# Three edits to a planned attention and two-layer kernel: work that POOL may take, copies left out, and sums that start without their scale

## The chip, the cores and the metric

The kernel runs on one core of a Trainium2 chip. The core has five engines with a queue each: TensorE (PE, with its weight loads shown apart as PEld), VectorE (DVE), ScalarE (ACT), GpSimd (POOL) and SyncE (SP), which here only issues DMAs. Each queue is worked off in order; an instruction at its head that waits holds up all that is behind it. The metric is the device time of one execution in microseconds (us); less is better. Three runs of the kernel before gave 1190.7, 1194.28 and 1189.9 us, median 1190.7.

## The reference

Three stages follow one another. Attention on 4 batches, 8 heads, 768 positions of 64 values, in chunks of 32 queries: each chunk sees 8 memory keys and its own keys with 16 to the left and 8 to the right, and the softmax is normalised. Its output, seen as 3072 tokens of 512 values, goes through a layer with a leaky rectifier, and that through a layer with a product of two branches:

```
a = np.exp(scores);  a = a / (np.sum(a, axis=-1, keepdims=True) + 1e-09)
x = (a @ v_full), all heads side by side: 3072 x 512
h = x @ w_in                                  # 512 x 2048
g = np.maximum(h, 0.0) + alpha * np.minimum(h, 0.0)
y = g @ w_out                                 # 2048 x 512
out = ((y @ w_a) * (y @ w_b)) @ w_o2          # 512 x 1536, twice, and 1536 x 512
```

## The kernel before

**Products.** Every large product runs in 16 bits with both factors split into an upper and a lower half (hi and lo): three matmuls, hi by hi, hi by lo and lo by hi, add up in PSUM (`gemm3`, lines 910 to 912). A split is one ACT instruction (hi, line 347) and one DVE instruction (lo = value times scale minus hi, line 351). The scale of a split is a power of two found from the largest magnitude of the data (`scale`, lines 299 to 330: a transpose on PE, line 310, and short DVE instructions from line 315 on).

**First stage.** The attention works on 24 units of 128 tokens. Of one unit (`attention`): k and q are turned on PE (lines 716 and 705), scores (740), the largest of a row (DVE, 756), exponentials with their sums (ACT, 766), the reciprocal of the sums (DVE, 774 and 777), the normalisation `norm` in two halves, each by DVE (782) or by ACT (788, four instructions), the turn of the normalised weights (PE, 792), their copy (`p_evac`, 645 on DVE or 647 on ACT), and the product with v (806). Two or four units make a block of x; `gemm1` multiplies it with `w_in` in 16 pieces. Each piece leaves PSUM through ACT (lines 927 and 930) and DVE (933) and is split: hi on ACT (939), lo on DVE (942, in `lo_`). `gemm2` needs all pieces of the block. Beside this the weights are made from 64-bit words (`chunk`): c0 on ACT (531), c1, c4, c2 and c3 on DVE (537 or 541, 546, 553, 560), then the scale and the split. For the 18 pieces of `w_a`, `w_b` and `w_o2` (`pair` is true) POOL forms sums of four quarters (`sums`, line 367), since the last layer multiplies with 7 products in place of 8 (Winograd's form), and the split parts go to DRAM.

**Second stage.** Six blocks of 512 tokens (`second`). For each of six pieces j, `pair` multiplies y with `w_a` and `w_b` and forms the product of both (`both`, line 1298), whose largest magnitude ACT takes (1304). From the six maxima comes one scale `sp` for the block (1253 to 1258). `operands` then forms the sums of the quarters of each piece (four instructions of line 367, one after the other, on POOL, in the last block on POOL or DVE) and splits pieces and sums (line 347 on ACT, 351 on DVE, two each). `output` multiplies with `w_o2`; each of its 7 products runs over all six pieces. The sums go into one of two buffers `s32`, which comes free when the piece is split; the split parts go into `pu`.

**What sets the order.** Nothing is ordered by hand. `Schedule` takes all operations with a rank, the data that they read and write, and an assumed cost on each engine that may run them. `emit` then always issues the operation that can start first by these assumed times, with ties by rank and cost, and writes it into the queue of the engine that it chose. The order of every queue is therefore fixed when the program is built.

## Time and profile before

| what | value |
|---|---|
| median of three runs | 1190.7 us (1189.9 to 1194.28) |
| the profiled execution | 1191.92 us |
| its span, first to last instruction | 1190.2 us |
| PE busy | 1126.7 us, 95% |
| DVE busy | 868.6 us, 73% |
| ACT busy | 604.7 us, 51% |
| POOL busy | 226.5 us, 19% |

The profiled execution took 1.7 us more than its span, which lies around the program, and is 1.2 us above the median. Busy time is counted once where instructions overlap. An idle time is put down to what ended it. TensorE's clock has two levels, 2.4 and 1.2 GHz; the profile gives the granted clock as a share of the higher one.

### The profile page before, as it was taken

Reading aid. Unit: us, or ns where it says so; the run is one execution under the profiler, and the core shown is the slowest. Engines: PE = TensorE matmul, PEld = TensorE weight load, DVE = VectorE, ACT = ScalarE, POOL = GpSimd, SP = SyncE. Lnnn points to the kernel's source line nnn. Section 1 sums busy time; section 2 is a strip of 40 time slices with the busy share of each in tenths; the row PEclk is TensorE's granted clock in tenths of the full one; section 3 lists DMA queues with packets and bytes.
Section 4 is the critical chain, followed back from the end, with each engine's and each line's share of the span. In section 5 each row is a group of like instructions: output and inputs, shape, how many; then the busy total and the mean of one; then the engine's idle time right before and its main releaser. Section 6 shows DMA issues by size and latency. Waiting matters only on the chain.

```text
span 1190.2 us, 23137 instructions
## 1 busy us (share of the span) xinstructions
PE 1126.7 (95%) x9304; PEld 811.2 (68%) x9304; DVE 868.6 (73%) x1533; ACT 604.7 (51%) x1326; POOL 226.5 (19%) x293
## 2 busy tenths in 40 slices
PE   4399999999999999999999999999999999999988
PEld 3278886555445554444444588888888888888877
DVE  6989998987998799335243187886867958858881
ACT  4689778975886698246253032433424423324340
POOL 1000012111112212100300010242433414234130
PEclk9589999999999999899999999999999999999999
DMA  9935664647635633530103052512513514315101
GB/s 263 258 81 139 154 191 127 186 132 219 200 103 167 194 127 106 179 140 32 50 10 133 27 190 90 188 66 94 191 54 112 173 37 156 130 52 187 63 36 37
DMA packets 162523, 150.93 MB, mean 127 GB/s; under 512 B 104032, under 2 KB 139888, under 8 KB 162416
## 3 DMA queue, kind: packets, MB, share of 16 engines
q1 hardware_dynamic: 162416, 149.45, 41.5%
q8 instruction: 73, 1.20, 0.4%
q14 instruction: 34, 0.28, 0.1%
HBM read 120.33 MB, written 29.10 MB: 126 GB/s over the span
## 4 chain that ended last, share of the span: by engine, by line
PE 74%; DVE 13%; ACT 6%; DMA 3%; SPq 2%; issue 2%; ACTq 0%; DVEq 0%
PE mm L910 23%; PE mm L912 23%; PE mm L911 23%; ACT sm L766 2%; PE pair L792 2%; DVE ghl L942 1%; DVE g L933 1%; DVE w L553 1%; PE mm L806 1%; DMA qt<-in_q_dram 1%; SPq L688 1%; DVE nm L756 1%; DVE w L560 1%; ACT sp L347 1%; ACT t L930 1%
## 5 line engine op out<-in xcount | busy, mean ns | idle before, releaser
L912 PE MATMUL mm<-xhl,w 128*128 128x512 f16 (+1 forms) x448 | 157.3, 351 | 1.9 <-DVE w L553 1.9
L910 PE MATMUL mm<-xhl,w 128*128 128x512 f16 (+1 forms) x448 | 157.6, 352 | 0.3 <-ACT t L930 0.2
L912 PE MATMUL mm<-ghl,w 128*128 128x512 f16 (+1 forms) x448 | 156.9, 350 | 0.9 <-DVE w L351 0.9
L911 PE MATMUL mm<-xhl,w 128*128 128x512 f16 (+1 forms) x448 | 157.4, 351 | 0.3 <-DVE xhl L351 0.3
L910 PE MATMUL mm<-ghl,w 128*128 128x512 f16 (+1 forms) x448 | 157.2, 351 | 0.0
L911 PE MATMUL mm<-ghl,w 128*128 128x512 f16 (+1 forms) x448 | 156.9, 350 | 0.0
L910 PE MATMUL mm<-units,w1b 128*128 128x256 f16 x560 | 153.4, 274 | 0.0
L911 PE MATMUL mm<-units,w1b 128*128 128x256 f16 x560 | 153.4, 274 | 0.0
L912 PE MATMUL mm<-units,w1b 128*128 128x256 f16 x560 | 153.3, 274 | 0.0
L912 PEld LDWEIGHTS <-w 128*128 128x128 f16 x896 | 88.2, 98 | 83.5 <-DVE w L553 2.2
L910 PEld LDWEIGHTS <-w 128*128 128x128 f16 x896 | 88.5, 99 | 75.5 <-issue 0.8
L911 PEld LDWEIGHTS <-w 128*128 128x128 f16 x896 | 88.3, 99 | 73.5 <-issue 1.7
L910 PE MATMUL mm<-w2b,w1b 128*128 128x256 f16 x504 | 137.4, 273 | 0.1
L912 PE MATMUL mm<-w2b,w1b 128*128 128x256 f16 x504 | 137.4, 273 | 0.0
L911 PE MATMUL mm<-w2b,w1b 128*128 128x256 f16 x504 | 137.4, 273 | 0.0
L910 PEld LDWEIGHTS <-w1b 128*128 128x128 f16 x1064 | 104.4, 98 | 13.0 <-DMA w1b<-wb_d 0.5
L911 PEld LDWEIGHTS <-w1b 128*128 128x128 f16 x1064 | 104.4, 98 | 12.7
L912 PEld LDWEIGHTS <-w1b 128*128 128x128 f16 x1064 | 104.4, 98 | 12.2
L367 POOL TENSOR_TENSOR raw<-w 128x256 f32<-128x256 f32 x18 | 16.1, 893 | 409.7 <-ACT raw L568 248.8
L933 DVE SCALAR_TENSOR_TENSOR g<-t,columns,g 128x512 f32<-128x512 f32 (+1 forms) x112 | 75.8, 683 | 24.3 <-ACT t L930 24.2
L942 DVE TENSOR_TENSOR ghl<-g,ghl 128x512 f16<-128x512 f32 (+1 forms) x112 | 70.8, 638 | 23.8 <-ACT ghl L939 23.4
L927 ACT ACTIVATE g<-mm 128x512 f32<-128x512 f32 (+1 forms) x112 | 60.5, 547 | 50.5 <-PE mm L912 48.4
(293 smaller groups left out, 2403.5 us busy)
## 6 DMA issues: line engine op xcount, KB each, us to landing
w1b<-wa_d SPq DMA_DIRECT2D x26, 896.0 KB
w1b<-wb_d SPq DMA_DIRECT2D x26, 896.0 KB
raw<-in_moe_w_out_dram SPq DMA_DIRECT2D x8, 1024.0 KB
kw<-in_k_dram SPq DMA_DIRECT2D x40, 176.0 KB
vw<-in_v_dram SPq DMA_DIRECT2D x40, 176.0 KB
qt<-in_q_dram SPq DMA_DIRECT2D x24, 256.0 KB
raw<-in_moe_w_a_dram SPq DMA_DIRECT2D x12, 512.0 KB
raw<-in_moe_w_b_dram SPq DMA_DIRECT2D x12, 512.0 KB
```

Of the source, the lines that this page charges most:

```text
L347: nc.scalar.activation(out=hi, in_=src, func=ACTF.Copy, scale=s)
L367: (nc.vector if e == "DVE" else nc.gpsimd).tensor_tensor(out=out_()[:, i], in0=x()[:, a], in1=y()[:, b], op=op)
L553: nc.vector.scalar_tensor_tensor(out=f, in0=lo, scalar=29, in1=f, op0=ALU.logical_shift_right, op1=ALU.bitwise_or)
L560: nc.vector.scalar_tensor_tensor(out=lo if nm == "w1" else f, in0=hi, scalar=KEEP, in1=f, op0=ALU.bitwise_and, op1=ALU.bitwise_or)
L766: nc.scalar.activation(out=sm.tile[:, o, g], in_=scored()[:, o, g], func=ACTF.Exp, bias=stat["nm"][:, i : i + 1], scale=1.0, accum_out=sta ...
L792: nc.tensor.transpose(out=heads(pp, P)[:KW, o, g], in_=sm.tile[:, o, g], identity=ident)
L910: nc.tensor.matmul(out=ps, lhsT=lh, rhs=rh, start=first and i == 0, stop=False)
L911: nc.tensor.matmul(out=ps, lhsT=lh, rhs=rl, start=False, stop=False)
L912: nc.tensor.matmul(out=ps, lhsT=ll, rhs=rh, start=False, stop=last and i == n - 1)
L927: nc.scalar.activation(out=g.tile[:, :n], in_=ps.tile[:, :n], func=ACTF.Relu, scale=E1)
L933: nc.vector.scalar_tensor_tensor(out=g.tile[:, :n], in0=t2.tile[:, :n], scalar=nal[:, m : m + 1], in1=g.tile[:, :n], op0=ALU.mult, op1=ALU ...
L942: nc.vector.tensor_tensor(out=ghl.tile[:, 1, m, d], in0=g.tile[:, :n], in1=ghl.tile[:, 0, m, d], op=ALU.subtract,)
```

## The change

There are three edits. `norm` may run on POOL as well as on DVE or ACT, and `lo_` of `gemm1` on POOL as well as on DVE, each with the planner's cost `pool(n)`. The inverse scale of the 18 pieces of `w_a`, `w_b` and `w_o2` is written straight to its place in `inv_w`, and the DVE copy that put it there (line 575) goes. In the last block of the second stage the sums of a piece wait for the piece and its maximum and no longer for the scale; the first two pieces take their sums' buffer from the larger `p32` buffers and their `pu` from `yu_slots`, the other four from `ring_slots`.

```diff
--- before.py
+++ after.py
@@ -510,7 +510,7 @@
         rk = raw_key(c) if nm == "w1" else (raw, 0)
         w32 = "w32w1" if nm == "w1" else Buf(w32_slots)
         fk = ("w32w1", c) if nm == "w1" else (w32, 0)
-        am, s, inv = (s_w1, s_w1, inv_w1) if nm == "w1" else (col(), col(), col())
+        am, s, inv = (s_w1, s_w1, inv_w1) if nm == "w1" else (col(), col(), inv_w[nm][:, c : c + 1] if pair else col())
         key = f"{nm}{c}"
 
         def load():
@@ -568,11 +568,8 @@
             nc.scalar.activation(out=t[:, :n], in_=w32.tile[:, :n], func=ACTF.Abs, accum_out=am)
 
         def after():
-            if nm == "w2":
-                r = slice(c % 2 * CR, (c % 2 + 1) * CR)
-                nc.vector.tensor_copy(out=inv_w2[r, c // 2 : c // 2 + 1], in_=inv[r])
-            else:
-                nc.vector.tensor_copy(out=inv_w[nm][:, c : c + 1], in_=inv)
+            r = slice(c % 2 * CR, (c % 2 + 1) * CR)
+            nc.vector.tensor_copy(out=inv_w2[r, c // 2 : c // 2 + 1], in_=inv[r])
 
         sd.op("SP", dma(n * 8 * P), load_rank, load, (), [rk])
         sd.op("ACT", act(n), rank, c0, [rk], [fk])
@@ -591,7 +588,7 @@
             sd.op("ACT", act(n, 2), rank, sizes, [fk], [rk, (key + "am", 0)])
             scale(
                 lambda: am, s, inv, [(key + "am", 0)], [(key + "s", 0), (f"inv_{nm}{c}", 0)],
-                rank=rank - 0.3, after=[after],
+                rank=rank - 0.3, after=[after] if nm == "w2" else [],
             )
         def scaled():
             src = [rk, ("s_w1", 0)] if nm == "w1" else [(w32, 0), (key + "s", 0)]
@@ -778,8 +775,8 @@
 
         def norm(e, o):
             rs = stat["rs"][:, o * HP : (o + 1) * HP]
-            if e == "DVE":
-                nc.vector.tensor_tensor(
+            if e != "ACT":
+                (nc.vector if e == "DVE" else nc.gpsimd).tensor_tensor(
                     out=sm.tile[:, o], in0=sm.tile[:, o],
                     in1=rs[:, :, None].to_broadcast([P, HP, KW]), op=ALU.mult,
                 )
@@ -839,7 +836,7 @@
         sd.op("DVE", 0.09, rank, part_of, [], [(sm, 2)])
         for o in range(2):
             sd.op(
-                None, {"DVE": dve(n), "ACT": 4 * act(KW, 1) + 0.15}, rank, lambda e, o=o: norm(e, o),
+                None, {"DVE": dve(n), "ACT": 4 * act(KW, 1) + 0.15, "POOL": pool(n)}, rank, lambda e, o=o: norm(e, o),
                 [(sm, 2), (sm, 0)], [(sm, ("n", o))],
             )
             sd.op("PE", 4 * pe(P, 2), prank, lambda o=o: p_turn(o), [(sm, ("n", o))], [(pp, o)])
@@ -938,8 +935,8 @@
         def hi_():
             nc.scalar.copy(out=ghl.tile[:, 0, m, d], in_=g.tile[:, :n])
 
-        def lo_():
-            nc.vector.tensor_tensor(
+        def lo_(e):
+            (nc.vector if e == "DVE" else nc.gpsimd).tensor_tensor(
                 out=ghl.tile[:, 1, m, d], in0=g.tile[:, :n], in1=ghl.tile[:, 0, m, d],
                 op=ALU.subtract,
             )
@@ -955,7 +952,9 @@
         sd.op("ACT", act(n), er, below, [(ps, 0)], [(t2, 0)])
         sd.op("DVE", dve(n, pointers=1), er, both, [(t2, 0), ("alpha", 0)], [(g, 0)])
         sd.op("ACT", act(n), er, hi_, [(g, 0)], [(ghl, ("h", m, c0))])
-        sd.op("DVE", dve(n), er, lo_, [(g, 0), (ghl, ("h", m, c0))], [(ghl, (m, c0))])
+        sd.op(
+            None, {"DVE": dve(n), "POOL": pool(n)}, er, lo_, [(g, 0), (ghl, ("h", m, c0))], [(ghl, (m, c0))]
+        )
 
     def gemm2(jb, m, ghl, c0, n, iy, rank):
         ps, y32 = Buf(mm_slots), Buf(g_slots)
@@ -1172,13 +1171,14 @@
                 keys += [("yd", j, m) for m in range(KD)]
         return keys
 
-    def operands(r, b, h, s, reads, cost):
-
-        o = Buf(s32_slots)
+    def operands(r, b, h, s, reads, cost, ready=None, slots_=None):
+
+
+        o = Buf(slots_ or s32_slots)
         unit = lambda: b.tile
-        others = lambda: o.tile
-
-        sd.op("POOL", 0.0, r, lambda: None, reads, [(h, "held")], holds=[h])
+        others = lambda: o.tile[:, :3]
+
+        sd.op("POOL", 0.0, r, lambda: None, reads if ready is None else ready, [(h, "held")], holds=[h])
         sums(
             r, b, o, [(b, 0), (h, "held")], [],
             [
@@ -1261,10 +1261,14 @@
             lambda: am1, sp, io, [(f"amp1{jb}", 0), ("ratio", 0)], [(f"sp{jb}", 0)], after=after
         )
 
-        pu = {j: Buf((ring_slots if i < 4 else yu_slots) if last_ else pu_slots) for i, j in enumerate(js)}
+        pu = {j: Buf((yu_slots if i < 2 else ring_slots) if last_ else pu_slots) for i, j in enumerate(js)}
         cost = {"POOL": pool(HT), "DVE": dve(HT)} if last_ else {"POOL": pool(HT)}
         for j in js:
-            operands(r, ps[j], pu[j], lambda j=j: spj[:, j : j + 1], [(f"sp{jb}", 0), (ps[j], 0)], cost)
+            operands(
+                r, ps[j], pu[j], lambda j=j: spj[:, j : j + 1], [(f"sp{jb}", 0), (ps[j], 0)], cost,
+                [(ps[j], 0), ("amp", jb, j)] if last_ else None,
+                p32_slots if last_ and j in list(js)[:2] else None,
+            )
         for tt in range(HT // P):
             output(jb, tt, pu, io, r + 30)
 
```

Since the planner chooses anew at each step, the queues change everywhere in the first stage. Three places follow. The lines of `attention` and `gemm1` have numbers lower by 3 in the changed kernel.

PE, where the first stage's products begin, in the kernel before; `qt` is a unit's q, `xhl` the split x and `w_94` the split `w_in`:

```order
L740 MATMUL pair<-kT,qT 64x96 x16
L310 MATMUL mm<-ident,columns 128x128 x2
L705 MATMUL mm<-ident,qt 128x128 x4
L910 LDWEIGHTS w_94
L910 MATMUL mm<-xhl,w_94 128x256
L911 LDWEIGHTS w_94
L911 MATMUL mm<-xhl,w_94 128x256
L912 LDWEIGHTS w_94
L912 MATMUL mm<-xhl,w_94 128x256
```

The same place in the changed kernel:

```order
L737 MATMUL pair<-kT,qT 64x96 x16
L310 MATMUL mm<-ident,columns 128x128 x2
L907 LDWEIGHTS w_94
L907 MATMUL mm<-xhl,w_94 128x256
L908 LDWEIGHTS w_94
L908 MATMUL mm<-xhl,w_94 128x256
L909 LDWEIGHTS w_94
L909 MATMUL mm<-xhl,w_94 128x256
```

The turn of the third unit's q, which stood ahead of the first product, now stands behind its twelve matmuls (four groups of three).

POOL, behind the masks that it writes at the start, in the kernel before; `raw` and `w_2098` hold a piece of `w_a`:

```order
L294 MEMSET mask_88 32x32
L298 MEMSET mask_88 32x8
L367 TENSOR_TENSOR raw<-w_2098 128x256
L367 TENSOR_TENSOR raw<-w_2098,raw 128x256
L367 TENSOR_TENSOR w_2098<-w_2098 128x256
```

The same place in the changed kernel, up to the first sum:

```order
L294 MEMSET mask_88 32x32
L298 MEMSET mask_88 32x8
L779 TENSOR_TENSOR sm<-sm,rs 128x384 x3
L939 TENSOR_TENSOR ghl<-g,ghl 128x256 x3
L779 TENSOR_TENSOR sm<-sm,rs 128x384 x2
L939 TENSOR_TENSOR ghl<-g,ghl 128x256 x5
L779 TENSOR_TENSOR sm<-sm,rs 128x384
L939 TENSOR_TENSOR ghl<-g,ghl 128x256 x5
L779 TENSOR_TENSOR sm<-sm,rs 128x384
L939 TENSOR_TENSOR ghl<-g,ghl 128x256 x8
L779 TENSOR_TENSOR sm<-sm,rs 128x384 x3
L367 TENSOR_TENSOR raw<-w_2067 128x256
```

In the whole program POOL gets 23 halves of the normalisation (line 779, 384 elements to a partition) and 43 lower halves (line 939; 21 of 256 elements and 22 of 512). DVE loses 12 halves of the normalisation, the same 43 lower halves and the 18 copies; ACT loses 44 instructions of the normalisation (11 halves). Three copies of k move from ACT to DVE, and three copies of weights from DVE to ACT.

DVE behind the last block's scale (line 1258), in the kernel before; `x_6475`, `quarters`, `w1b` and `xhl` as inputs of line 367 are pieces, `s_...` the buffers of sums, `cb` an output of the block before:

```order
L1258 TENSOR_TENSOR columns<-columns 128x1
L421 SCALAR_TENSOR_TENSOR cb<-mm_12826,columns,g 128x512
L367 TENSOR_TENSOR s_12936<-quarters 128x256
L427 SCALAR_TENSOR_TENSOR cb<-mm_12826,columns,cb 128x256
L367 TENSOR_TENSOR x_6475<-x_6475 128x256
L367 TENSOR_TENSOR s_12916<-s_12916,x_6475 128x256
L367 TENSOR_TENSOR s_12936<-s_12936,quarters 128x256
L433 SCALAR_TENSOR_TENSOR cb<-mm_12891,columns,cb 128x512
L351 SCALAR_TENSOR_TENSOR w1b<-x_6475,columns,w1b 128x1024
L415 SCALAR_TENSOR_TENSOR cb<-mm,columns,cb 128x256
L351 SCALAR_TENSOR_TENSOR w1b<-s_12916,columns,w1b 128x768
L351 SCALAR_TENSOR_TENSOR w1b<-quarters,columns,w1b 128x1024
```

The same place in the changed kernel:

```order
L1258 TENSOR_TENSOR columns<-columns 128x1
L421 SCALAR_TENSOR_TENSOR cb<-mm_12784,columns,g 128x512
L427 SCALAR_TENSOR_TENSOR cb<-mm_12784,columns,cb 128x256
L351 SCALAR_TENSOR_TENSOR units<-x_6412,columns,units 128x1024
L433 SCALAR_TENSOR_TENSOR cb<-mm_12858,columns,cb 128x512
L351 SCALAR_TENSOR_TENSOR units<-w2b,columns,units 128x768
L351 SCALAR_TENSOR_TENSOR units<-quarters,columns,units 128x1024
L415 SCALAR_TENSOR_TENSOR cb<-mm,columns,cb 128x256
L351 SCALAR_TENSOR_TENSOR units<-ghl,columns,units 128x768
L351 SCALAR_TENSOR_TENSOR w1b<-x_6412,columns,w1b 128x1024
L409 SCALAR_TENSOR_TENSOR g<-mm,columns,cb 128x256
L351 SCALAR_TENSOR_TENSOR w1b<-s_12671,columns,w1b 128x768
```

Behind the scale DVE had twelve sums of line 367 among its twelve splits; now it has three, all further down, and four pieces have their sums ahead of the scale.

## Rows read from the trace of the kernel before

**Rows 1.** Windows: stretch, length, PE, PEld, DVE, ACT, POOL busy, PE clock, DMA

```profile
0.00:62.00 62.00, 25.77 (x231) 18.96 (x232) 48.94 (x86) 35.01 (x85) 4.97 (x41) 0.74 0.95 256
62.00:500.00 438.00, 420.44 (x3694) 264.93 (x3693) 377.80 (x722) 332.17 (x868) 64.68 (x73) 0.99 0.54 152
300.00:360.00 60.00, 55.43 (x399) 29.49 (x398) 56.16 (x97) 51.98 (x130) 7.40 (x8) 1.00 0.52 149
1152.00:1164.00 12.00, 7.45 (x43) 4.92 (x41) 7.80 (x11) 4.00 (x5) 1.55 (x2) 0.72 0.10 35
```

**Rows 2.** Waits of PE, 0 to 62 us: us in total, times, longest

```profile
PE pair L792 <- DVE sm L782: 11.9, 2, 7.0
PE mm L705 <- DMA qt<-in_q_dram: 10.3, 1, 10.3
```

**Rows 3.** Timeline, DVE and PE before the first product: start, duration, instruction

```profile
21.51 0.69 DVE L645 COPY pT<-pair 96x512 f32<-96x512 f32 x1 [1.11 <-PE pair L792]
...
34.42 1.03 DVE L782 TENSOR_TENSOR sm<-sm,rs 128x384 f32<-128x384 f32 x2
...
57.64 1.42 DVE L351 SCALAR_TENSOR_TENSOR xhl<-x,columns,xhl 128x512 f16<-128x512 f32 x2 [0.24 <-ACT xhl L347]
...
60.24 1.09 PE L705 MATMUL mm<-ident,qt 128*128 128x128 f32 x4 [10.33 <-DMA qt<-in_q_dram]
```

**Rows 4.** Groups by form, DVE and ACT, whole span: busy us, mean ns | idle

```profile
L942 DVE TENSOR_TENSOR ghl<-g,ghl 128x512 f16<-128x512 f32 x80 | 58.1, 728 | 23.0 <-ACT ghl L939 22.6
...
L782 DVE TENSOR_TENSOR sm<-sm,rs 128x384 f32<-128x384 f32 x32 | 17.5, 571 | 0.6
...
L942 DVE TENSOR_TENSOR ghl<-g,ghl 128x256 f16<-128x256 f32 x32 | 12.7, 415 | 0.8 <-ACT ghl L939 0.8
...
L575 DVE COPY columns<-columns 128x1 f32<-128x1 f32 x18 | 2.4, 134 | 0.0
```

**Rows 5.** Groups by form, ACT, whole span

```profile
L788 ACT ACTIVATE sm<-sm,rs 128x96 f32<-128x96 f32 x64 | 18.7, 377 | 5.4 <-DVE rs L777 5.4
```

**Rows 6.** Groups by form, POOL, whole span

```profile
L367 POOL TENSOR_TENSOR raw<-w,raw 128x256 f32<-128x256 f32 x36 | 33.1, 920 | 1.3
...
L367 POOL TENSOR_TENSOR s<-s,x 128x256 f32<-128x256 f32 x12 | 8.7, 725 | 0.0
```

**Rows 7.** Timeline, POOL, in the last block

```profile
1136.36 0.72 POOL L367 TENSOR_TENSOR s<-quarters,s 128x256 f32<-128x256 f32 x1
1139.57 1.70 POOL L367 TENSOR_TENSOR s<-x 128x256 f32<-128x256 f32 x1 [2.48 <-DVE w1b L351]
```

**Rows 8.** Timeline, DVE, behind the last block's scale

```profile
1132.91 0.15 DVE L1258 TENSOR_TENSOR columns<-columns 128x1 f32<-128x1 f32 x1
...
1133.64 0.41 DVE L367 TENSOR_TENSOR s<-quarters 128x256 f32<-128x256 f32 x1
...
1136.47 1.70 DVE L351 SCALAR_TENSOR_TENSOR w1b<-x,columns,w1b 128x1024 f16<-128x1024 f32 x1
...
1139.41 1.27 DVE L351 SCALAR_TENSOR_TENSOR w1b<-quarters,columns,w1b 128x1024 f16<-128x1024 f32 x1
1142.26 0.48 DVE L409 SCALAR_TENSOR_TENSOR g<-mm,columns,cb 128x256 f32<-128x256 f32 x1 [1.57 <-ACT cb L406]
...
1154.74 0.43 DVE L367 TENSOR_TENSOR s<-xhl,s 128x256 f32<-128x256 f32 x1
...
1157.21 1.28 DVE L351 SCALAR_TENSOR_TENSOR units<-xhl,columns,units 128x1024 f16<-128x1024 f32 x1
```

**Rows 9.** Timeline, PE, at the last block's first output product

```profile
1156.42 0.39 PE L912 MATMUL mm<-units 128*128 128x256 f16 x1 [3.25 <-DVE units L351]
...
1158.54 0.39 PE L912 MATMUL mm<-units 128*128 128x256 f16 x1 [1.30 <-DVE units L351]
...
1163.15 0.27 PE L910 MATMUL mm<-units,w1b 128*128 128x256 f16 x1
1163.26 0.27 PE L911 MATMUL mm<-units,w1b 128*128 128x256 f16 x1
```

## The prediction

> **What bounds the kernel.** I read the windows first, by stage, for where PE is not busy; then the waits of PE; then the timeline at the two largest; then the groups that the edits touch. PE works 1126.7 of 1190.2 us, so a change of its helpers can return no more than the 63.5 us in which it stands still, and what a low clock costs. Of the idle time 36.2 us lie before 62 us (62.0 less 25.8), 17.6 between 62 and 500 (438.0 less 420.4), and 4.6 between 1152 and 1164 [rows 1]. Before 62 us two waits stand out: 11.9 us for normalised weights and 10.3 us for the third unit's q [rows 2]. At the end it is two waits for the last piece's splits, 3.25 and 1.30 us [rows 9]. Of DVE the reader is to see that it is the nearest second: 377.8 of 438 us in the first stage, and 56.2 of 60 in the stretch from 300 us, where PE lost 4.6 us [rows 1]. POOL has room: 64.7 of 438.
>
> **The end: sums without the scale.** Before, nothing of the six pieces could start until the scale was there at 1133.06 (1132.91 and 0.15), and the first half of the last piece was ready at 1158.49 (1157.21 and 1.28) [rows 8]. In these 25.4 us DVE did twelve splits, eight instructions of the output of the block before, and twelve sums, of which the first and the last took 0.41 and 0.43 us [rows 8]. In the new order three of the twelve sums are left behind the scale. Nine sums at 0.42 are 3.8 us; some of them were held up beside POOL, so I take 4.2. The other way to the same place: DVE waited 1.57 us for a product of PE at 1142.26 [rows 8], and PE's place in that product does not change, so the new order reaches that point, does five splits ahead of it where it did three, and goes on at 1142.7. Behind it stand seven splits (three of 1.27 us as at 1139.41, four of three quarters of that size, 0.95: 7.6), four outputs (two as at 1142.26, 0.48, two twice as wide, counted at 0.7: 2.4) and the three sums (1.3): 11.3 us, which would end at 1154.0 were nothing waited for, the first half of the last piece 0.95 earlier. But the two last pieces take their sums' buffers from the third and the fourth, so five POOL instructions of 0.73 [rows 6] stand in between, in a chain with those three sums; I give this 1.2 us. So 1154.3, which is 4.2 earlier. PE comes to that operand at 1153.17 (1156.42 less 3.25), and its two waits of 4.55 us become one of about 1.1: 3.4 gained. From both sides: 0, if the POOL chain is late by 4 us more, and 4.55.
>
> Behind the wait PE ran at the lower clock level, until 1163: between 1152 and 1164 the granted clock is 0.72 and 43 matmuls took 7.45 us [rows 1]; at the step of 0.11 us between 1163.15 and 1163.26 [rows 9] they take 4.7. That is 2.7 us, which goes if the level holds through a wait of 1.1 us. No row shows that for certain; I take two thirds, 1.8. The end gives 5.2 us, with 0 and 7.2 as its bounds. The held buffers cost nothing that I can see: `yu_slots` has two units free in the last block, and the ring's units come free with the pieces whose product is done. What the earlier sums stand in front of on POOL is only other sums; on DVE one of 0.42 us comes ahead of the last `both`, and the transpose for the scale is tied to its place in PE's queue anyway.
>
> **The start: norm on POOL.** Before the first product DVE loses one copy of weights (0.69) and one of two normalisations (1.03 for both) [rows 3]: 1.2 us. The split x was ready at 59.06 (57.64 and 1.42), but PE stood at the turn of q until 60.24, for its DMA [rows 3]. In the new order twelve matmuls come first, and the q is there by the time that they end. So PE starts at 59.1 if DVE gains nothing and at 57.9 if it gains all: 1.1 to 2.3 us earlier. POOL's own halves are longer than those they replace (below), and one of them is in the chain of 11.9 us [rows 2], so the lower bound is 0; I take 1.6.
>
> **The middle: DVE and ACT against POOL.** Removed from DVE: 22 lower halves of 0.728, 21 of 0.415, 12 normalisations of 0.571 and 18 copies of 0.134 [rows 4]: 16.0, 8.7, 6.9 and 2.4, in all 34.0 us. From ACT: 44 of 0.377 [rows 5], 16.6 us. The copies that change sides are three each way, about nothing. Added to POOL: the trace has no such instruction of POOL. Its sums of 256 elements take 0.725 us undisturbed and 0.92 in the first stage [rows 6]. For 512 elements the bounds are 0.73 (no growth) and 1.84 (twice the slow one); I take 1.4, and for 384 by the same line 1.05. So 21 at 0.73, 22 at 1.4 and 23 at 1.05: 70.3 us, with which POOL is busy some 135 of 438 us, which it can be. No queue is held up for that but POOL's own: sums of the weight pieces stand behind it, and they have until the second stage.
>
> But the two engines get in each other's way. At 1136.36 POOL worked for 0.72 us, and DVE's split of 1136.47 took 1.70 in place of 1.27; at 1139.41 DVE's split began first, took its 1.27, and POOL's sum of 1139.57 took 1.70 in place of 0.72 [rows 7, 8]. Each time the later one ends as if it had begun when the other was done. On the average POOL pays 0.2 us an instruction (0.92 less 0.725) [rows 6]; for DVE I take as much, an estimate: 66 new instructions, 13 us. DVE keeps a relief of 21 us in 378, ACT 17 in 332.
>
> The Trainium skill says this harder (SBUF — State Buffer, section "Who interferes with whom"): DVE and GpSimd share a pair of ports that is an exclusive lock, a DVE instruction with two inputs in SBUF takes part in it when GpSimd reads SBUF, and the one that comes second blocks fully. The two collisions above agree. By that rule every microsecond moved to POOL could cost DVE as much, which is the second rival below.
>
> PE's 17.6 us of waits in the middle are many small ones. With less on DVE and ACT they shrink; with a slower engine inside the attention's chain and a wholly new order some come anew. Bounds: 10 us better (more than half gone) and 20 worse (below). I take 1.5 better, close to nothing, since the nearest row, the stretch with PE 55.4 and DVE 56.2 of 60 [rows 1], shows that both bind there.
>
> **The sum.** 5.2, 1.6 and 1.5 are 8.3 us. The profiled execution took 1191.9 (span 1190.2 and 1.7 around it): 1183.6. It lay 1.2 above the median of its runs, so the time to compare with that median is 1182.4. About 0.5%, 6 us, is what can be told from no change: below 1184.7 is faster, above 1196.7 slower.
>
> **Rivals.** *The order wins more.* The end returns all of 7.2, the start 2.3, the middle 5: 14.5 us, so 1176. For it: planner and chip agree on a DVE with 9% less to do. Against: PE's queue is as strict as before.
>
> *POOL shuts DVE out.* One mechanism, in the first stage: POOL's 66 instructions hold what DVE's two-input instructions need. If DVE pays the full 70.3 us, it goes from 377.8 to 414 of 438, 95%, about PE's own share. The stretch from 300 us shows the price of that: DVE at 94%, PE idle 4.6 of 60 [rows 1]; over 438 us that is 33.6 in place of 17.6, 16 worse, and if half of POOL's longer latencies come on top, 20. With the gains of 6.8 elsewhere it ends 9 to 13 above 1190.7, near 1201. It decides from the point where DVE pays more than 34.0 us, 0.5 an instruction. For it: the collisions are complete. Against: POOL's sums have paid only 0.2 each, and DVE's reductions and its readings of PSUM go on beside POOL.
>
> *The end does not come.* The chain of POOL sums for the last two pieces is so late that PE waits as long as before and the clock falls as before; start and middle give 3.1 or are lost to a new wait: 1188 to 1191, no change. For it: the two `s32` buffers tie the last pieces to the splits of the third and fourth. Against: nine sums fewer on the engine that was late.
>
> **From here to the chances.** The forecast 0.43, the larger gain 0.21, no gain at the end 0.26, POOL's lock 0.10. The forecast's own range, 1179 to 1187, lies for three quarters below 1184.7. Faster: 0.33 and 0.21, 0.54. Same: the rest of the forecast and the third rival, 0.36. Slower 0.10. The range for 8 in 10 leaves out most of the lock and the far end of the larger gain: 1174 to 1193.
>
> **What would show it.** Right at the end: PE's two waits by the last units' splits of 1.5 us or less in sum, and three sums on DVE behind the scale. Right at the start: the first product near 58.5 us. Right in the middle: DVE near 357 us of the same 438, its two-input instructions hardly longer on the average, PE idle near 16. Wrong: lower halves on DVE that last over 1 us beside POOL's, POOL's own at over 2 us, PE waiting for normalised weights from POOL, or the lower clock level still behind the last scale.

## The result, and the profile after

The changed kernel takes 1204.4 us in the median of four runs, against 1190.5; the ratio of the runs is 1.0101, with a 95% interval from 1.0086 to 1.0117. The forecast was 1182.4, with a range of 1174 to 1193. The kernel became slower where it was to become faster. The profiled execution has a span of 1202.3 us, 12.1 more than before.

The windows of the changed kernel, columns as in [rows 1]:

```profile
0.00:62.00 62.00, 29.19 (x243) 21.09 (x244) 49.31 (x84) 35.90 (x87) 8.86 (x44) 0.67 0.95 256
62.00:500.00 438.00, 406.10 (x3568) 255.25 (x3567) 377.47 (x638) 324.21 (x819) 141.95 (x134) 0.98 0.54 149
300.00:360.00 60.00, 55.82 (x399) 29.76 (x396) 54.78 (x89) 43.92 (x110) 28.35 (x25) 0.97 0.63 189
1152.00:1164.00 12.00, 12.00 (x113) 10.76 (x111) 10.62 (x13) 8.02 (x9) 1.30 (x1) 1.00 0.12 45
```

PE is busy through the whole of the last stretch, at the full clock; before it had 7.45 of 12 at 0.72. From 62 to 500 it stands still for 31.9 us (438.0 less 406.1) where it was 17.6. DVE is as busy as before, 377.5 and 377.8, with 84 instructions fewer. Two places of PE's timeline show both ends, the number in brackets being the idle time before:

```profile
57.08 0.37 PE L907 MATMUL mm<-xhl,w 128*128 128x256 f16 x1 [10.19 <-ACT xhl L347]
...
1172.88 0.28 PE L909 MATMUL mm<-units,w1b 128*128 128x256 f16 x1 [0.66 <-DVE w1b L351]
```

PE goes on at 57.08, 3.2 us earlier than at 60.24 [rows 3]; the two waits of 4.55 us by the last splits [rows 9] have become one of 0.66. So start and end gave more than forecast, the end some 6.6 (3.9 of waits and the 2.7 of the low clock), and about 22 us were lost between (12.1, 3.2 and 6.6). The waits of PE from 62 to 500 us (in total, times, longest) say where:

```profile
PE mm L310 <- ACT raw L568: 13.2, 13, 2.3
PE pair L789 <- DVE sm L779: 3.1, 3, 1.3
PE mm L310 <- DVE columns L874: 3.0, 3, 1.4
...
PE pair L789 <- POOL sm L779: 0.7, 1, 0.7
```

In the kernel before the first of these was:

```profile
PE mm L310 <- ACT raw L568: 2.0, 3, 0.8
```

It is the transpose of a weight piece's maximum (`scale`), which stands in PE's queue and waits for ACT's maximum, and this for DVE's four instructions that put the piece's words together. PE hardly waits for POOL. The groups of DVE by form answer to [rows 4] (busy us, mean ns | idle):

```profile
L939 DVE TENSOR_TENSOR ghl<-g,ghl 128x512 f16<-128x512 f32 x58 | 42.9, 739 | 36.4 <-ACT ghl L936 36.4
...
L779 DVE TENSOR_TENSOR sm<-sm,rs 128x384 f32<-128x384 f32 x20 | 13.6, 679 | 0.5
L939 DVE TENSOR_TENSOR ghl<-g,ghl 128x256 f16<-128x256 f32 x11 | 6.6, 605 | 0.0
```

The groups of POOL by form answer to [rows 6]:

```profile
L367 POOL TENSOR_TENSOR raw<-w,raw 128x256 f32<-128x256 f32 x36 | 35.0, 973 | 1.3
L939 POOL TENSOR_TENSOR ghl<-g,ghl 128x512 f16<-128x512 f32 x22 | 30.3, 1376 | 165.5 <-ACT ghl L936 165.3
L779 POOL TENSOR_TENSOR sm<-sm,rs 128x384 f32<-128x384 f32 x23 | 26.4, 1149 | 155.4 <-DVE rs L774 66.1 <-DMA vw<-in_mem_v_dram 25.2 <-ACT raw L568 17.1
L939 POOL TENSOR_TENSOR ghl<-g,ghl 128x256 f16<-128x256 f32 x21 | 20.7, 988 | 48.9 <-ACT ghl L936 48.8
```

POOL's 66 instructions took 77.4 us (estimated: 70.3). DVE's normalisation went from 571 to 679 ns and its lower halves of 256 from 415 to 605. One place shows how such a delay reaches PE, in the timeline of all engines:

```profile
377.01 0.74 DVE L930 SCALAR_TENSOR_TENSOR g<-t,columns,g 128x512 f32<-128x512 f32 x1
...
377.21 3.65 POOL L939 TENSOR_TENSOR ghl<-g,ghl 128x512 f16<-128x512 f32 x2 [1.28 <-ACT ghl L936]
...
379.77 1.64 DVE L930 SCALAR_TENSOR_TENSOR g<-t,columns,g 128x512 f32<-128x512 f32 x1
...
381.45 0.62 ACT L936 CAST ghl<-g 128x512 f16<-128x512 f32 x1 [0.56 <-DVE g L930]
...
384.03 1.04 ACT L568 ACTIVATE raw<-w 128x1024 bf16<-128x1024 f32 x1
...
385.22 0.32 PE L310 MATMUL mm<-ident,columns 128*128 128x128 f32 x1 [2.33 <-ACT raw L568]
```

The same DVE instruction takes 0.74 us and, next to POOL's pair, 1.64; ACT idles 0.56 us before its upper half, the maximum stands behind three more instructions on ACT, and PE waits 2.33 us. So of these 2.33 us, 0.56 come visibly from this one delay; for the rest the place shows no single cause. The first section of the profile's page counts it all up:

```profile
PE 1131.8 (94%) x9304; PEld 811.7 (68%) x9304; DVE 871.3 (72%) x1455; ACT 598.3 (50%) x1282; POOL 315.6 (26%) x364
```

### The profile page after: what moved, and what is told of

It is laid out like the page before. It is cut to its first block, busy times and chain, and to the rows that moved or that the text cites. A ratio compares the mean times of both kernels' runs of the same rounds, so it can differ in the third digit from the quotient of the medians.

```text
span 1202.3 us, 23165 instructions
## 1 busy us (share of the span) xinstructions
PE 1131.8 (94%) x9304; PEld 811.7 (68%) x9304; DVE 871.3 (72%) x1455; ACT 598.3 (50%) x1282; POOL 315.6 (26%) x364
## 4 chain that ended last, share of the span: by engine, by line
PE 68%; DVE 20%; ACT 6%; issue 4%; DMA 2%; SPq 1%; POOL 0%; ACTq 0%; DVEq 0%; POOLq 0%
PE mm L907 22%; PE mm L908 22%; PE mm L909 22%; DVE g L930 3%; DVE w L560 2%; DVE w L553 2%; ACT sm L763 2%; DVE w L541 1%; DVE sp L351 1%; DVE nm L753 1%; PE pair L789 1%; DVE w L546 1%; DVE ghl L939 1%; DVE columns L812 1%; DMA kw<-in_k_dram 1%
## 5 line engine op out<-in xcount | busy, mean ns | idle before, releaser
L907 PE MATMUL mm<-xhl,w 128*128 128x512 f16 (+1 forms) x448 | 158.9, 355 | 10.4 <-ACT xhl L347 10.2
L939 POOL TENSOR_TENSOR ghl<-g,ghl 128x512 f16<-128x512 f32 (+1 forms) x43 | 51.0, 1186 | 214.4 <-ACT ghl L936 214.2
L930 DVE SCALAR_TENSOR_TENSOR g<-t,columns,g 128x512 f32<-128x512 f32 (+1 forms) x112 | 83.7, 753 | 29.6 <-ACT t L927 29.4
L936 ACT CAST ghl<-g 128x512 f16<-128x512 f32 (+1 forms) x112 | 62.0, 561 | 52.0 <-DVE g L930 51.8
```

Source lines behind the costliest of these rows:

```text
L907: nc.tensor.matmul(out=ps, lhsT=lh, rhs=rh, start=first and i == 0, stop=False)
L930: nc.vector.scalar_tensor_tensor(out=g.tile[:, :n], in0=t2.tile[:, :n], scalar=nal[:, m : m + 1], in1=g.tile[:, :n], op0=ALU.mult, op1=ALU ...
L936: nc.scalar.copy(out=ghl.tile[:, 0, m, d], in_=g.tile[:, :n])
L939: (nc.vector if e == "DVE" else nc.gpsimd).tensor_tensor(out=ghl.tile[:, 1, m, d], in0=g.tile[:, :n], in1=ghl.tile[:, 0, m, d], op=ALU.sub ...
```

## The experiments

Three theories. A: POOL's instructions hold DVE up, and that is the loss. B: the loss is in the new order, whatever runs where. C: the results come later from POOL than from DVE. Times are medians; "before" was run on the same chip each time, with medians from 1192.1 to 1193.4, so ratios are what to compare. One per cent is 11.9 us.

**The edits one by one.** First the last block's edit alone in the kernel before (`operands` and `pu` as changed, all else old):

> The kernel before with the edit of the last block alone; the queues of the first stage are those of before, instruction for instruction. The changed kernel's trace had no wait and no low clock left at the end, 4.55 and 2.7 us less. So every theory expects 1183 to 1185, about 6.6 us below before. If it is 1187 or more, part of what vanished at the end of the changed kernel vanished because its last block came at another time, and the middle then cost less than 24 us.

1186.5 us, ratio 0.9952 (0.9937 to 0.9967): 5.7 us gained, on the end alone; the 6.6 of the trace lie within the interval. Next the changed kernel with fewer choices for POOL:

```diff
-None, {"DVE": dve(n), "ACT": 4 * act(KW, 1) + 0.15, "POOL": pool(n)}, rank, lambda e, o=o: norm(e, o),
+None, {"DVE": dve(n), "ACT": 4 * act(KW, 1) + 0.15}, rank, lambda e, o=o: norm(e, o),
-None, {"DVE": dve(n), "POOL": pool(n)}, er, lo_,
+"DVE", dve(n), er, lo_,
```

Both lines changed:

> The changed kernel without POOL as a choice for the normalisation and the lower halves; the copies stay out and the sums of the last block begin early. The planner orders the first stage anew, as it does for any change. Theory A (POOL's instructions hold DVE up) expects 1182 to 1186. Theory B (a new order is itself worse, whatever runs where) expects a loss of some size here too, 1190 or more.

The first alone:

> The changed kernel with POOL as a choice for the lower halves alone: 57 of them (25 of 256, 32 of 512 elements), at the changed kernel's durations 25 x 0.99 and 32 x 1.38, 69 us of POOL. The changed kernel lost about 24 us in the middle with 77 us on POOL. Theory A (the loss goes with POOL's time, since DVE is held up) expects 21 us of loss, 1200 to 1205. Theory C (POOL's long instruction lies in the chain of the attention, from the sums to the turn of the weights) expects most of the loss gone: 1183 to 1190.

The second alone:

> The changed kernel with POOL as a choice for the normalisation alone: 22 halves of 1.15 us, 25 us of POOL. Theory A expects a third of the loss, 8 us: 1188 to 1193. Theory C expects nearly all of it: 1198 to 1205. If only the edit of the end and the start's gain stood, it would be 1181.

No POOL: 1191.3, 0.9990 (0.9978 to 1.0002). Lower halves only: 1205.0, 1.0109 (1.0094 to 1.0124). Normalisation only: 1192.4, 0.9989 (0.9977 to 1.0001). Without POOL 4.5 us are lost against the end's edit alone, by an order that only 18 copies fewer have made: a first sign of B. The normalisation costs next to nothing beside that, so C as I put it falls; 1192.4 lies in the range that A gave, but as much is lost with no POOL at all. The lower halves alone make the whole loss. Each of the three is also an order of its own, so by themselves they cannot tell POOL's part from the order's.

**Order and engine apart.** The order of the changed kernel with the old engines; tables written out from the two plans say which engine that is (the tables are shortened to a name here and below):

```diff
+e = ENGINE_BEFORE[iu, o]   # in norm
+e = "DVE"                  # in lo_
```

> The changed kernel with its order, but the engines of before: the planner still plans with POOL, each operation keeps the place in the program that this plan gives it, and the 43 lower halves run on DVE and the 48 halves of the normalisation on the engines that they had before. Theory A (POOL's work holds DVE up) expects the loss gone: 1185 to 1192, as without POOL as a choice. Theory B (the new order is the fault) expects 1200 to 1206, or worse, since DVE now has the work that the order was made without.

Then the old order with the changed kernel's engines, by tables in the same two places:

> The opposite: the order of before (with the edit of the last block, 1186.5) and its 18 copies, but each of the same 66 operations (43 lower halves, 23 halves of the normalisation) runs on POOL, at its old place in the program. Theory A expects most of the 18 us between that kernel and the changed one: 1198 to 1206, and the wait of PE's transposes for ACT's maximum, 2.3 us, to grow to 10 or more. Theory B expects 1184 to 1189, since nothing is reordered and DVE is relieved of 33 us.

And the old order with nothing moved, but POOL kept at work beside it:

```diff
+if on_pool_after[jb, m]:
+    nc.gpsimd.tensor_tensor(out=idle_b[:, :n], in0=ghl.tile[:, 0, m, d], in1=ghl.tile[:, 0, m, d], op=ALU.subtract)
```

> The kernel before with the edit of the last block, and nothing moved: beside it POOL does 43 subtractions more, of the upper halves that it has been given in the changed kernel from themselves (16 bit, same sizes and places), into a scratch buffer that nobody reads. So DVE keeps all its work and no one waits for POOL. If the time is lost because DVE is held up while POOL works (theory A), DVE's instructions get longer by 0.3 to 0.4 us for each, 13 to 17 us in the first stage, and the kernel comes to 1194 or more. If it is lost because the result comes later from POOL than from DVE (theory C), it stays at 1186 to 1188.

Order only: 1205.0, 1.0102 (1.0081 to 1.0122). POOL only: 1191.2, 0.9985 (0.9973 to 0.9997), far from A's range but 2 us above B's too. Idle work on POOL: 1203.3, 1.0090 (1.0066 to 1.0113). The first is A's defeat in its simple form: with none of the 66 operations on POOL the loss is as large as with all of them, and the same wait leads, in the waits of PE from 62 to 500 us of that kernel:

```profile
PE mm L310 <- ACT raw L568: 12.8, 13, 2.0
```

It even begins its products nearly as early (57.47 us), so most of the start's gain is one of the order too. But the third shows that POOL's hold on DVE is real: with the old order and nothing moved, it alone costs 16.4 us (1.0090 less 0.9952). The page's first section of order only:

```profile
PE 1130.6 (94%) x9304; PEld 811.3 (67%) x9304; DVE 870.1 (72%) x1510; ACT 608.6 (51%) x1326; POOL 240.9 (20%) x298
```

That of POOL only:

```profile
PE 1127.5 (95%) x9304; PEld 811.2 (68%) x9304; DVE 860.2 (72%) x1473; ACT 595.5 (50%) x1282; POOL 314.0 (26%) x364
```

That of the idle work:

```profile
PE 1128.5 (94%) x9304; PEld 811.9 (68%) x9304; DVE 885.1 (74%) x1528; ACT 607.2 (51%) x1326; POOL 290.4 (24%) x341
```

And that of the end's edit alone, with which the last two compare:

```profile
PE 1124.5 (95%) x9304; PEld 810.0 (68%) x9304; DVE 867.0 (73%) x1528; ACT 604.8 (51%) x1326; POOL 232.0 (20%) x298
```

Idle work of 43 instructions makes DVE 18.1 us busier (885.1 less 867.0), 0.42 each. In the old order 31.6 us moved off DVE (34.0 without the copies) relieve it by 6.8: 24.8 are paid back, 0.38 for each of 66. In the new order the same move relieves it by nothing: 871.3 against 870.1, so about 33 paid back, 0.50 each. So order only and the changed kernel have the same busy DVE and the same time. In the old order the move costs 0.33% (0.9985 less 0.9952), 3.9 us, though DVE is a little freer: that much may be C, which is not shown.

**The wait itself.** The wait for the maxima as the place of the loss:

```diff
-sd.op("ACT", act(n, 2), rank, sizes, [fk], [rk, (key + "am", 0)])
+sd.op("ACT", act(n, 2), rank, sizes, [fk], [rk, (key + "am", 0)], late=3.0)
```

> The changed kernel with one number for the planner: what reads a weight piece's maximum (the transpose in PE's queue) is planned 3 us later. POOL keeps 71 operations. In the changed kernel PE waited 13.2 us for these maxima. If that wait is where the time is lost, it goes and the kernel comes to 1190 to 1195. If the wait is only the place where a DVE that is late everywhere shows first, other waits take its place: 1200 to 1205.

1214.1, 1.0174 (1.0147 to 1.0200). The leading waits of PE from 62 to 500 us are now:

```profile
PE pair L713 <- ACT pT L644: 7.1, 1, 7.1
PE pair L789 <- DVE sm L779: 5.8, 4, 3.0
PE mm L803 <- DVE m L315: 5.5, 1, 5.5
```

The wait for the maxima went and others came, which fits a wait that is only the place where lateness shows first. It is not proof: this is one more new order, and it came out slower than both expectations.

**Theory D.** What do bad orders have in common? Adding up the costs by which the planner places DVE's instructions between 62 and 480 us of its own clock gives 359 us for the old order and 331 for the changed kernel's, with 43 lower halves, a dozen normalisations and the 18 copies counted as gone. (By the planner's clock that is nearly all of DVE's work of this stage: the 20 us behind 480 hold 1.4 us of it in the old order.) The chip's DVE is busy for 377 to 378 from 62 to 500 us in either. D says: the order is planned for a DVE that the chip doesn't have, PE's queue is packed by it, and each step of DVE comes later than PE's next place in the queue. If so, the same order is good once DVE's load really falls. In both orders the 23 halves of the normalisation are left out, the 43 lower halves are zeros from DVE, and all else runs on the engines of before:

```diff
+if normalised_on_pool_after[iu, o]: return                                    # in norm
+if on_pool_after[jb, m]: return nc.vector.memset(ghl.tile[:, 1, m, d], 0.0)   # in lo_
```

> The order of the changed kernel once more, and POOL without the new work, but now DVE really has little to do: the 23 halves of the normalisation that went to POOL are left out, and of the 43 lower halves DVE only writes zeros. Theory D: the order was made for a DVE with 27 us less to do than in the order of before, and any DVE that has not (because it does the work itself, or because POOL holds it up) misses its places in the queues; by it the time falls to 1181 to 1190. Theory B (this order is bad in itself, whatever DVE has to do) expects 1198 or more.

> The same work left out (23 halves of the normalisation, 43 lower halves written as zeros) in the order of before with the edit of the last block, 1186.5. This says what a relief of DVE is worth at best where the order stays: theory D expects 1178 to 1185, since an order made for a busier DVE has slack in every place but is not denser; if it stays at 1186, DVE's load was no part of what PE waited for in that order.

The changed order: 1186.7, 0.9955 (0.9937 to 0.9973), 17.5 us below order only. The old order: 1178.1, 0.9874 (0.9856 to 0.9892), 9.3 below its own. Both are as D expected. So the order isn't bad whatever DVE has to do; relief is worth about twice as much in it. But the old one stays 9.6 us better under the same load, with PE's wait for maxima at 1.5 us against 8.5. Its plan had counted some 27 us more for DVE. The first section of the changed order's page:

```profile
PE 1120.2 (95%) x9304; PEld 808.1 (68%) x9304; DVE 851.8 (72%) x1500; ACT 594.5 (50%) x1274; POOL 241.0 (20%) x298
```

Against order only DVE is relieved of 18.3 us (870.1 less 851.8), but ACT of 14.1 too (608.6 less 594.5), since 13 of the 23 halves were ACT's, and no turn of the weights waits for those halves any more. So the two runs show what relief of both engines is worth, not of DVE alone.

Two other ways to a new order, DVE charged for POOL's work, and DVE counted 0.03 us longer for each instruction:

```diff
 free[e] = t + cost
+if e == "POOL" and len(o.costs) > 1 and t < 480.0:
+    free["DVE"] = max(free["DVE"], t) + 0.5
```

> The changed kernel, but the planner charges DVE 0.5 us for each operation of the first stage that it gives to POOL where it had a choice. It still puts 54 lower halves and 21 halves of the normalisation there. Theory D expects the order to fit again: 1184 to 1192. Theory A in its simple form (POOL's time on DVE is what costs, whatever the order) expects 1200 to 1206, with 75 operations on POOL. Theory B expects any of the values seen for new orders with POOL, 1200 to 1215.

```diff
-return 0.07 + 0.06 * pointers + n * rate / 1000
+return 0.10 + 0.06 * pointers + n * rate / 1000
```

> The kernel before with the edit of the last block, POOL without new work, and a planner that counts each DVE instruction 0.03 us longer (its sum for 62 to 480 us rises from 359 to 368 us; the chip has 378). The first stage is ordered anew. Theory D expects it no worse than the old order, 1182 to 1187; theory B, in which a new order costs 4 us or more by itself (the kernel without POOL as a choice lost 4.5), 1190 or more.

Charged: 1197.1, 1.0037 (1.0020 to 1.0055): two fifths of the 17.7 us between the changed kernel and the end's edit are back. D expected 1192 at most, A and B 1200 at least; it lies between. The other: 1207.1, 1.0113 (1.0085 to 1.0141), a miss for D. Its windows show that most of it is another matter, since that number counts in the second stage as well:

```profile
62.00:500.00 438.00, 415.95 (x3673) 261.91 (x3672) 372.65 (x712) 336.68 (x881) 64.94 (x73) 0.99 0.56 156
500.00:1132.00 632.00, 620.41 (x4813) 471.98 (x4812) 399.62 (x658) 217.69 (x350) 138.49 (x164) 0.99 0.31 102
1132.00:1165.00 33.00, 28.88 (x243) 24.62 (x241) 30.32 (x44) 12.96 (x17) 16.38 (x17) 0.90 0.05 17
```

PE loses 11.6 us from 500 to 1132, where the kernels above lose 1.4 to 2.8, and 4.1 up to 1165. Behind 500 us it waits five times for DVE's split of a piece; the end's edit alone has one such wait, of 0.8:

```profile
PE mm L912 <- DVE ghl L351: 14.1, 5, 3.0
```

So the next runs scale DVE's cost in the first stage only, `f` being 1.05, 0.92, 1.14 (changed kernel) and 1.10:

```diff
 (_, _, cost, t), e, o = best
+if e == "DVE" and t < 470.0:
+    cost *= f
```

> The kernel before with the edit of the last block (1186.5), no new work on POOL, and a planner that counts DVE's instructions of the first stage 5% longer; the second stage is planned as it was. Its sum for DVE from 62 to 480 us is 375 us where the old order had 359 and the chip takes 378. Theory D (what counts is how far the order's DVE is from the chip's) expects 1180 to 1187. Theory B (a new order from this planner is a draw, and the old one was a lucky one) expects something between 1188 and 1207.

> The same with DVE's instructions counted 8% shorter: the planner's DVE has 333 us there, as in the changed kernel (331), and the chip's has 378 or so. POOL has no new work and no operation may go there. Theory D expects the changed kernel's loss without POOL: 1200 to 1208. Theory A (POOL's work is what costs) expects 1184 to 1190.

> The changed kernel with POOL as a choice (55 lower halves go there) and DVE's instructions of the first stage counted 14% longer, so that the planner's DVE has 366 us where the changed kernel's had 331 and the chip's 377. Theory D expects most of the 18 us back: 1184 to 1193. Theory A expects 1200 to 1207, with as much of POOL's work as before or more.

> As the first of these four, with 10% longer: the planner's DVE has 381 us, a little more than the chip's. Theory D expects 1180 to 1188; theory B a draw between 1188 and 1207.

| kernel | planner's DVE, us | ratio (interval) | PE's wait for maxima, us and times |
|---|---|---|---|
| end's edit, 0.92 | 333 | 1.0069 (1.0046 to 1.0092) | 10.8, 10 |
| end's edit, 1 | 359 | 0.9952 (0.9937 to 0.9967) | 2.3, 3 |
| end's edit, 1.05 | 375 | 0.9917 (0.9888 to 0.9947) | 4.3, 6 |
| end's edit, 1.10 | 381 | 1.0001 (0.9985 to 1.0017) | 2.7, 6 |
| changed kernel, 1 | 331 | 1.0101 (1.0086 to 1.0117) | 13.2, 13 |
| changed kernel, 1.14 | 366 | 1.0041 (1.0025 to 1.0057) | 2.5, 3 |

A plan with a light DVE costs 13.9 us with no new work on POOL at all (1.0069 less 0.9952), and the leading wait is that of the changed kernel; in the waits of PE of that kernel (its lines are higher by 2):

```profile
PE mm L312 <- ACT raw L570: 10.8, 10, 2.3
```

This is what D expected (1199.8, a hair under its 1200) and A excluded. A heavier DVE in the changed kernel's plan takes back 7.1 us and nearly all of that wait, less than D expected: with 55 lower halves on POOL it stays 10.6 us above the end's edit and 6.1 above no POOL (1.0041, 0.9952 and 0.9990). POOL's own part may be in that, but it is not shown: one wait of PE alone, for a split of weights on ACT (line 349), takes 6.4 us. With 1.10 the planner's DVE has more to do than the chip's (381, and 372 from 62 to 500); it missed what D expected by 4.6 us, and 1.05 (375, and 379) is the better.

The planner's own clock tells more than DVE's sum in it. By that clock the end's edit ends at 1165.0 us, with 1.05 at 1169.3, with 1.10 at 1178.7, with 0.92 at 1162.6, the changed kernel at 1164.3, and the kernel with 0.03 us more for each instruction at 1191.9. Their spans on the chip are longer than that by 21.2, 10.9, 14.9, 33.9, 38.0 and 14.4 us. A plan with a light DVE is short and is not kept; one with a heavy DVE is kept better, but is itself longer, in part simply because its costs are higher. The loss of the last kernel was in its plan already. So D bears on how far the chip falls behind a plan, and does not say which plan is best.

**A better version.** The last two runs join what helped; the first also lets POOL normalise in the first four units (`{...} | ({"POOL": pool(n)} if iu < 4 else {})`, `f` 1.05), the second has `f` 1.03:

> A version that should beat both kernels: the edit of the last block, DVE counted 5% longer in the first stage (1181.6 with these two), and POOL as a choice for the normalisation of the first four units only, where the changed kernel began its first product 3 us earlier and POOL has no other work. Theory D expects the start's gain on top where the rest of the order fits as well: 1178 to 1183. If each new order is a draw of its own beside the fit (theory B in part), 1180 to 1190.

> The edit of the last block and DVE counted 3% longer (the planner's DVE has 371 us from 62 to 480; 359 gave 1186.5, 375 gave 1181.6). Theory D expects 1181 to 1187, between the two. Anything above 1188 is the size of the draw that theory D leaves unexplained.

1183.2, 0.9920 (0.9904 to 0.9936), with the first product at 57.18, a hair above what D expected; and 1191.0, 0.9989 (0.9972 to 1.0005), clearly above. Both known neighbours of that point are 4 to 9 us faster: that is the size of the draw between orders that nothing here explains. The best is the end's edit with `f` 1.05: 1181.6 us, 0.8% faster than before and 1.8% faster than the changed kernel (0.9917 and 1.0101); the start's edit on top is not told apart from it.

Of its ten expectations D met three, missed two by 0.2 us, and missed five by more. What holds in all runs is weaker: without new work on POOL the two orders planned for a light DVE, order only (1.0102) and `f` 0.92 (1.0069), are slower than the five planned for a DVE of 357 us or more with the second stage left alone (0.9917 to 1.0001).

## Why the prediction was wrong

**The end** was right. 5.2 us forecast, 5.7 measured by itself (3.9 to 7.5). One wait of 0.66 us stayed where I had 1.1, and the clock stayed at its full level there (1.00 from 1132 to 1165 us with the end's edit alone), for which I had counted two thirds.

**The start** had the right sign and half the size: 1.6 forecast, 3.2 by the timeline. I tied what was over 1.1 to DVE's relief by `norm` on POOL. Order only, without that, starts at 57.47: 2.8 of the 3.2 were the order.

**The middle** failed, at the step "DVE keeps a relief of 21 us in 378". POOL's price on DVE was put at 0.2 us an instruction, what POOL itself pays on the average; it is 0.38 to 0.50, so the relief is 7 us in the old order and nothing in the new. The Trainium skill says that the second to come blocks fully (SBUF — State Buffer, section "Who interferes with whom"). The pair at 379.77 looks so: DVE's instruction ends 0.55 us after POOL's two, a little less than the 0.74 us that it took before. Over all, 25 us were paid for 82 more of POOL in the old order (314.0 less 232.0) and 33 for 75 in the new (315.6 less 240.9), 30% and 44%.

What the relief would have been worth can be read from the changed order with the work left out: DVE is busy for 851.8 us there, 16.8 less than before, and ACT 10.2 less, and the kernel takes 0.9955, 5.4 us less than before (3.2 to 7.5). That is not far from the 8.3 of the sum, and 0.9955 of 1190.5 us, 1185, lies in the forecast's own range. As far as that run can stand for it (nothing waits for POOL in it), the forecast failed with the relief, and the relief with POOL's price.

The second fault is what made the missing relief so dear. I took the new order as neutral, with waits that "come anew" only as a bound of 20 us. But an order is planned by assumed loads. This one was packed for a DVE with some 27 us less to do, and order only shows its price when DVE has the whole load: 1.0102 against 0.9952, 17.9 us, with all the work back on its old engines. Moving the work to POOL then changed nothing, 1.0101. In PE's account against the end's edit alone this is 8.8 us more idle time (70.5 and 61.7, span less busy; the start's gain is already taken off), and 7.3 more busy time for the same 9304 matmuls (1131.8 and 1124.5). A part of the latter is the clock, which was seen to fall behind waits; how much was not separated. Between 386 and 394 us, behind the wait of 2.33, the changed kernel's window reads:

```profile
386.00:394.00 8.00, 6.47 (x42) 3.47 (x38) 7.08 (x13) 4.69 (x8) 3.60 (x4) 0.57 0.79 206
```

0.57 is little over the lower level, 0.5.

**The rival "POOL shuts DVE out"** named the price, 1201, and the point from which it decides, 0.5 an instruction, which POOL's price in the new order reaches. That the time came near is luck all the same, since the path was another: DVE never reached 95% (377.5 of 438 is 86%), and the changed order is as slow with none of the work on POOL. It is enough that DVE is later than its order supposes.

**Of the signs named beforehand**, DVE "near 357 us" failed first (377.5). Normalised weights from POOL were waited for 0.7 us only, so that sign of a loss was the wrong one to look for.

Open: why orders with like sums for DVE differ by 4 to 9 us; how much of the 3.9 us of the old order with POOL is POOL's later results; how much of the gain in the two runs with work left out is ACT's; and why the idle work on POOL cost 16.4 us (359 us planned for DVE, 389 taken from 62 to 500), while the changed order with work left out, as far from its plan (331 and 363), is as fast as the end's edit alone.

## What to carry to other kernels

Where an order is fixed when the program is built, an edit that moves work is two edits, the work and the order; run each without the other before either is believed. Beware of a plan that counts a busy engine too light: 8% lighter cost 13.9 us here. Counting it heavier is no sure remedy: against the end's edit, 3% cost 4.4 us, 5% won 4.2 (with intervals that touch) and 10% cost 5.8, so measure several orders before one is taken, and don't read a single new order as the effect of an edit. And when an elementwise instruction goes from DVE to POOL, count 0.38 to 0.50 us that come back on DVE, as here; where that is what DVE took for it, nothing is relieved.

## What the runs showed of the hardware

POOL's time grows with the number of elements: its lower halves of 256 and 512 took 988 and 1376 ns on the average, the shortest 0.67 and 1.15 us. Two lines of the changed kernel's timeline, among its shortest of their kinds, for 256 and 384:

```profile
65.14 0.67 POOL L939 TENSOR_TENSOR ghl<-g,ghl 128x256 f16<-128x256 f32 x1 [4.13 <-ACT ghl L936]
...
202.90 1.11 POOL L779 TENSOR_TENSOR sm<-sm,rs 128x384 f32<-128x384 f32 x1 [5.38 <-ACT sp L347]
```

With two 16-bit inputs POOL was no faster on the average. The groups by form of the kernel with idle work on POOL:

```profile
L948 POOL TENSOR_TENSOR idle_b<-ghl 128x512 f16<-128x512 f16 x22 | 34.7, 1575 | 153.3 <-ACT ghl L940 153.3
...
L948 POOL TENSOR_TENSOR idle_b<-ghl 128x256 f16<-128x256 f16 x21 | 21.4, 1018 | 102.0 <-ACT ghl L940 101.5
```

They stand against 1376 and 988 ns in the changed kernel. While these 56 us of POOL's work ran, DVE became 18.1 us busier.
